# A decode attention kernel: P stored head by head, P V over tokens 64 apart, a row sum moved by one place, and a new order of the last projection

## Chip, cores and metric

The kernel runs on one core of a Trainium2 chip. The metric is the device time in microseconds (us) of one execution. A program on one core gives no second die to compare with, so the state of a run is judged against the fastest run of the same kernel.

## The reference, cut to what matters

Eight tokens (B = 8) each attend to 4096 cached positions in 32 heads of size 128; beside that runs a small MLP, and a gate mixes the two.

```python
q = (x @ wq).reshape(B, 1, 32, 128).transpose(0, 2, 1, 3)
scores = einsum("bhqd,bhkd->bhqk", q, k_cache) * 128 ** -0.5
p = softmax(scores); o = einsum("bhqk,bhkd->bhqd", p, v_cache)
a = o.transpose(0, 2, 1, 3).reshape(B, 1, 4096) @ wo
b = gelu(layernorm(x) @ w1 + b1) @ w2 + b2
out = g * a + (1 - g) * b          # g = sigmoid(sum(x * gate_w))
```

K and V are 268 MB each in bf16; with the weights the kernel reads 557 MB.

## The kernel before

The work is cut into 32 groups (8 heads of one batch entry). A group's K is 8.4 MB: 128 partitions (16 for each of 8 heads) with 256 tokens of 128 values, 64 KB a partition. V is the same. There are three slots of that size in the on-chip memory; the loads go round them in the order K0, K1, V0, K2, V1, K3, V2, ... A load is issued when the slot it needs has been given up.

In the profiles PE is TensorE (PEld its weight loads), DVE is VectorE, ACT is ScalarE, and SP is the engine that issues the loads. For each group DVE multiplies K by q in 8 chunks; TensorE sums each chunk over the head size (8 matmuls with the identity per chunk, into PSUM); DVE reduces the rest. Then a short chain of DVE operations finds the maxima, ScalarE does 8 exps (one per head, with a bias that leaves only that head's own partitions above zero), and 64 matmuls form P V with the weights P (4 tokens x 8 heads = 32 columns) and V (4 tokens x 128) as the moving operand. P V of group g - 1 stands in TensorE's order after the scores of group g. Then three short steps follow: gather (TensorE adds up the row sums and the parts of the four tokens), norm (DVE divides by the row sum) and, after every fourth group, turn (TensorE transposes O for the projection with wo).

```python
HB = 8; NTT = 256; TQ = 4; NTQ = NTT // TQ        # heads, tokens per partition, tokens per matmul
P = sb("P", [128, NTT, HB], BF16)

# softmax(g), its last part
for h in range(HB):
    a_exp[g] = op("scalar", lambda e, h=h: e.activation(
        out=P[:, :, h], in_=s_sb[:, s, :], func=ACT.Exp, bias=hb8[:, h:h + 1], scale=1.0),
        [v_nm[g], p_pv.get(g - 1), v_rs.get(g - 1)])

def rowsum(g):       # DVE: sum of P over 2048 elements a partition; waits for the exps
    v_rs[g] = op("vector", lambda e: e.tensor_reduce(out=rr[...], in_=P[:, :, :]..., ...), [a_exp[g], ...])

def pv(g):
    for tq in range(NTQ):
        w = [land["v", g], a_exp[g], ...] if tq == 0 else ()
        p_pv[g] = op("tensor", lambda e, o=o, tq=tq: e.matmul(
            o, lhsT=P[:, tq * TQ:(tq + 1) * TQ, :].rearrange("p t h -> p (t h)"),
            rhs=vb[:, tq * TQ:(tq + 1) * TQ, :].rearrange("p t d -> p (t d)"), ...), w)

for g in range(NG):
    def between(c, g=g):                  # called after the multiply of chunk c
        if g >= 1 and c == 1:
            rowsum(g - 1)
        if g >= 2:                        # gather, norm (and every fourth group turn) of g - 2
            ...
    scores(g, between)                    # mult 0, mult 1, then: reduce c, mult c + 2
    free[n_of["k", g]] = [p_sum[g, NCK - 1]]      # K's slot: free after its last sums
    next_load() if g < NG - 1 else load_wo(...)   # this is where V of group g is issued
    if g >= 1:
        pv(g - 1)
        free[n_of["v", g - 1]] = [p_pv[g - 1]]
        next_load()                               # K of group g + 2
    softmax(g)
    ...
# ... cut ...
rowsum(last); pv(last); evict(last)
for m in range(6):                        # 96 of the 128 matmuls of the projection
    ...quarters(OT[:, m, r, :], wo_sb[:, m, ...], ...)
gather(last); norm(last); turn(last // 4)
for m in range(6, WM):                    # the other 32
    ...
```

Of the kernel before, what the change touches and what calls it, by code (L numbers as in the profile page):

```python
# [5 lines left out]
ACT = mybir.ActivationFunctionType  # L6
ALU = mybir.AluOpType
AX = mybir.AxisListType
BF16 = mybir.dt.bfloat16
F32 = mybir.dt.float32  # L10

B = 8
D = 576
H = 32
DH = 128
# [6 lines left out]
HB = 8  # L22
# [3 lines left out]
NTT = SK // PH  # L26
# [4 lines left out]
TQ = 4  # L31
NTQ = NTT // TQ
# [5 lines left out]
WM = H // 4  # L38
WR = 4
# [51 lines left out]
def bass_gated_mix__mha_block_cached__mixer_channel_mlp__decode_kernel(  # L91
# [16 lines left out]
    sb = nc.alloc_sbuf_tensor  # L108
    S = Stream(nc)
    op = S.op  # L110
# [21 lines left out]
    wo_sb = view(SL, WO_SLOT * SLOT, [128, WM, WR * D])  # L132
# [43 lines left out]
    OT = sb("OT", [128, WM, WR, B], BF16)  # L176
# [3 lines left out]
    ident = sb("ident", [128, 128], BF16)  # L180
    hsel = sb("hsel", [128, HB], F32)
    hneg = sb("hneg", [128, HB], F32)
    sel32 = sb("sel32", [128, TQ, HB], F32)
    stat = sb("stat", [B, 16], F32)
    s_sb = sb("s_sb", [128, 2, NTT], F32)
    mA = sb("mA", [128, 32], F32)
# [2 lines left out]
    mD = sb("mD", [128, 32], F32)  # L189
    gm = sb("gm", [128, 2], F32)  # L190
    hb8 = sb("hb8", [128, HB], F32)
    P = sb("P", [128, NTT, HB], BF16)
    rr = sb("rr", [128, 2], F32)
    O_sb = sb("O_sb", [128, TQ, DH], F32)
    rz = sb("rz", [128, 1], F32)
# [6 lines left out]
    oz_ps = bank[5]  # L202
# [71 lines left out]
    def own_head(t, inside, outside):  # L274
# [9 lines left out]
    c_ps = [memset("vector", bank[i][:, :], 0.0) for i in (0, 1, 4, 5, 6)]  # L284
    c_yps = memset("vector", y_ps[:, :], 0.0)
    c_sel32 = op("vector", lambda e: e.tensor_reduce(
        out=sel32[:].rearrange("p t h -> p (t h)"),
        in_=bass.AP(tensor=ident, offset=0, ap=[[pstride(ident), 128], [1, TQ * HB], [32, 4]]),
        axis=AX.X, op=ALU.add), [c_id])
    c_Sel = op("vector", lambda e: e.tensor_copy(  # L290
        out=Sel[:].rearrange("p b (h r) -> p b h r", h=4),
        in_=bass.AP(tensor=ident, offset=0, ap=[[pstride(ident), 128], [1, B], [32, 4], [0, PH]])), [c_id])


    t = op("vector", lambda e: e.tensor_reduce(out=stat[:, 0:1], in_=x_sb, axis=AX.X, op=ALU.add), [ld_x])
    t1 = op("vector", lambda e: e.tensor_tensor_reduce(out=junk, in0=x_sb, in1=x_sb, scale=1.0, scalar=0.0,
                                                       op0=ALU.mult, op1=ALU.add, accum_out=stat[:, 1:2]))
    t = op("vector", lambda e: e.tensor_scalar(out=stat[:, 2:3], in0=stat[:, 0:1], scalar1=1.0 / D, scalar2=None,
                                               op0=ALU.mult), [t])
    t = op("vector", lambda e: e.tensor_tensor(out=stat[:, 3:4], in0=stat[:, 2:3], in1=stat[:, 2:3], op=ALU.mult), [t])  # L300
# [33 lines left out]
    t = op("vector", lambda e: e.reciprocal(out=stat[:, 7:8], in_=stat[:, 5:6]), [a_sqrt])  # L334
# [13 lines left out]
    for half in range(2):  # L348
        for h in range(4):
            for kt in range(NKT):  # L350
                o = tr_ps[half][32 * h:32 * h + B, :]
# [51 lines left out]
    def quarters(lhsT, w, first, stop, waits):  # L403

        for i in range(4):
            last = op("tensor", lambda e, i=i: e.matmul(  # L406
                y_ps[32 * i:32 * i + B, 0:QN], lhsT=lhsT, rhs=w[:, i * QN:(i + 1) * QN], start=first, stop=stop),
                waits if i == 0 else ())
        return last
# [53 lines left out]
    def softmax(g):  # L463
        s = g % 2
        t = op("vector", lambda e: e.tensor_reduce(out=mA[:, 0:1], in_=s_sb[:, s, :], axis=AX.X, op=ALU.max),  # L465
               [v_red[g, NCK - 1], c_mA])
        t = op("vector", lambda e: e.transpose(mB[:, :], mA[:, :]), [t])
        t = op("vector", lambda e: e.tensor_reduce(out=gm[:, :], in_=mB[:, :].rearrange("p (k r) -> p k r", k=2),
                                                   axis=AX.X, op=ALU.max), [t])
        gmb = bass.AP(tensor=gm, offset=0, ap=[[pstride(gm), 128], [1, 2], [0, PH]])  # L470
        t = op("vector", lambda e: e.tensor_scalar(out=mC[:, :].rearrange("p (k r) -> p k r", k=2), in0=gmb,
                                                   scalar1=-1.0, scalar2=None, op0=ALU.mult), [t])
        t = op("vector", lambda e: e.transpose(mD[:, :], mC[:, :]), [t])
        v_nm[g] = op("vector", lambda e: e.tensor_scalar(out=hb8[:, :], in0=hneg[:, :], scalar1=mD[:, 0:1], scalar2=None,  # L474
                                                         op0=ALU.add), [t, c_hneg, a_exp.get(g - 1)])
        for h in range(HB):
            a_exp[g] = op("scalar", lambda e, h=h: e.activation(  # L477
                out=P[:, :, h], in_=s_sb[:, s, :], func=ACT.Exp, bias=hb8[:, h:h + 1], scale=1.0),
                [v_nm[g], p_pv.get(g - 1), v_rs.get(g - 1)])

    def rowsum(g):
        v_rs[g] = op("vector", lambda e: e.tensor_reduce(  # L482
            out=rr[:, g % 2:g % 2 + 1], in_=P[:, :, :].rearrange("p t h -> p (t h)"), axis=AX.X, op=ALU.add),
            [a_exp[g], p_z.get(g - 2)])

    def pv(g):
        s = g % 2
        vb = slot[at_slot["v", g]]
        for tq in range(NTQ):
            o = o_ps[s][32 * (tq % 4):32 * (tq % 4) + TQ * HB, :]  # L490
            w = [land["v", g], a_exp[g], a_ev.get(g - 2), *v_hT] if tq == 0 else ()
            p_pv[g] = op("tensor", lambda e, o=o, tq=tq: e.matmul(  # L492
                o, lhsT=P[:, tq * TQ:(tq + 1) * TQ, :].rearrange("p t h -> p (t h)"),
                rhs=vb[:, tq * TQ:(tq + 1) * TQ, :].rearrange("p t d -> p (t d)"),
                start=(tq < 4), stop=(tq >= NTQ - 4)), w)

    def evict(g):
# [6 lines left out]
    def gather(g):  # L504
        q = quad(g)
        p_z[g] = op("tensor", lambda e: e.matmul(  # L506
            oz_ps[q, DH:DH + 1], lhsT=hsel[:, :], rhs=rr[:, g % 2:g % 2 + 1], start=True, stop=True),
            [v_rs[g], v_norm.get(g - 4), c_hsel, *v_hb])
        for tt in range(TQ):
            p_oz[g] = op("tensor", lambda e, tt=tt: e.matmul(  # L510
                oz_ps[q, 0:DH], lhsT=sel32[:, tt, :], rhs=O_sb[:, tt, :], start=(tt == 0), stop=(tt == TQ - 1)),
                [a_ev[g], c_sel32] if tt == 0 else ())

    def norm(g):
        q = quad(g)
        t = op("vector", lambda e: e.reciprocal(out=rz[q, :], in_=oz_ps[q, DH:DH + 1]), [p_oz[g]])  # L516
        v_norm[g] = op("vector", lambda e: e.tensor_scalar(  # L517
            out=Orow[q, (g // 4) % 2, :], in0=oz_ps[q, 0:DH], scalar1=rz[q, 0:1], scalar2=None, op0=ALU.mult),
            [t, c_Or, p_tp.get(g // 4 - 2)])

    def turn(k):

        hg, b0 = divmod(4 * k, B)
        for r in range(WR):
            i = Orow[:, k % 2, r::WR]
            for h4 in range(4):
                p_tp[k] = op("tensor", lambda e, r=r, h4=h4, i=i: e.matmul(  # L527
                    tp_ps[32 * h4:32 * h4 + 32, r * 8:(r + 1) * 8], lhsT=i,
                    rhs=bass.AP(tensor=ident, offset=h4, ap=[[pstride(ident), 128], [4, 2], [32, 4]]),
                    start=True, stop=True), [v_norm[4 * k + 3], v_ot.get(k - 1), *v_hb] if r == h4 == 0 else ())  # L530
        v_ot[k] = op("vector", lambda e: e.tensor_copy(  # L531
            out=OT[:, 2 * hg:2 * hg + 2, :, b0:b0 + 4],
            in_=bass.AP(tensor=tp_ps, offset=0, ap=[[pstride(tp_ps), 128], [4, 2], [8, WR], [1, 4]])), [p_tp[k]])
# [20 lines left out]
    ld_wo = {}  # L554
# [10 lines left out]
    for g in range(NG):  # L565

        def between(c, g=g):
            if g >= 1 and c == 1:
                rowsum(g - 1)
            if g >= 2:  # L570
                if c == 2:
                    gather(g - 2)
                if c == 3:
                    norm(g - 2)
                if c == 4 and (g - 2) % 4 == 3:
                    turn((g - 2) // 4)
            if c == 5 and g + 1 < NG:
                q_of(g + 1)

        scores(g, between)  # L580
        free[n_of["k", g]] = [p_sum[g, NCK - 1]]
        if g < NG - 1:
            next_load()
        else:
            load_wo(free[n_of["k", g]])
# [3 lines that stand above are left out]
            next_load()  # L589
        softmax(g)  # L590
        if g >= 1:
            evict(g - 1)
    last = NG - 1
# [2 lines left out]
    rowsum(last)  # L596
    pv(last)
    evict(last)
    for m in range(6):
        for r in range(WR):  # L600
            p_a = quarters(OT[:, m, r, :], wo_sb[:, m, r * D:(r + 1) * D], m == r == 0, False,
                           [ld_wo[m, r], v_bx, *v_ot.values()])
    gather(last)
    norm(last)
    turn(last // 4)
    for m in range(6, WM):
        for r in range(WR):
            p_a = quarters(OT[:, m, r, :], wo_sb[:, m, r * D:(r + 1) * D], False, m == WM - 1 and r == WR - 1,
                           [ld_wo[m, r], v_ot[last // 4]])
    t = op("vector", lambda e: e.scalar_tensor_tensor(  # L610
        out=out_sb[0:QP, :], in0=y_ps[0:QP, 0:QN], scalar=g4[0:QP, 0:1], in1=bmg_sb[0:QP, :],
        op0=ALU.mult, op1=ALU.add), [p_a, v_bmg])
# [37 lines left out]
```

## Time and profile before

| | before |
|---|---|
| time, median of the first 3 runs | 1307.37 us (1307.22 to 1307.7) |
| bytes read, mean rate | 557.03 MB, 427 GB/s |
| share of the span in which the load queue was busy | 98.9% |
| busy: TensorE, DVE, ScalarE | 57%, 67%, 25% |

The page of the kernel before, from its part on DMA queues (packets, MB, share of 16 engines' span):

```profile
q1 hardware_dynamic: 11200, 556.93, 98.9%
HBM read 557.03 MB, written 0.01 MB: 427 GB/s over the span
```

The table by stretches, kernel before: the stretch in us and its length, busy us (and instructions) of PE, PEld, DVE, ACT and POOL, then the granted clock, the DMA share and GB/s.

```profile
122.00:1278.00 1156.00, 664.76 (x4270) 261.01 (x4266) 805.62 (x751) 301.94 (x299) 0.00 (x0) 0.85 1.00 433
...
114.00:116.00 2.00, 1.66 (x8) 0.70 (x8) 2.00 (x3) 0.00 (x0) 0.00 (x0) 1.00 1.14 492
116.00:118.00 2.00, 1.10 (x6) 0.41 (x5) 1.69 (x2) 0.00 (x0) 0.00 (x0) 1.00 0.00 0
118.00:120.00 2.00, 2.00 (x25) 0.85 (x27) 0.89 (x2) 0.00 (x0) 0.00 (x0) 1.00 0.00 0
120.00:122.00 2.00, 2.00 (x44) 0.97 (x36) 1.83 (x7) 0.00 (x0) 0.00 (x0) 1.00 1.52 524
```

The kernel is bound by its transfers, at 433 GB/s for over 1100 us, but there is one hole of 4 us near 116 us. (A packet is counted in the stretch in which it starts, so short stretches scatter around 433; only the zeros mean something: no packet started there.)

The timeline of the kernel before shows why. The lines are start, length, engine, source line, what; in brackets the idle time before it and what ended it. First ScalarE's 8 exps and DVE's row sum of group 0, then the load queue (SP): V of group 1 and K of group 3.

```profile
87.58 9.42 ACT L477 ACTIVATE P<-s_sb,hb 128x256 bf16<-128x256 f32 x8 [6.21 <-DVE hb L474]
97.03 2.29 DVE L482 TENSOR_REDUCE rr<-P 128x1 f32<-128x2048 bf16 x1 [5.09 <-ACT P L477]
...
119.07 0.33 SPq L259 DMA_DIRECT2D SL<-in_A_v_cache_dram  x1
122.65 0.33 SPq L259 DMA_DIRECT2D SL<-in_A_k_cache_dram  x1
```

DVE stands idle for 5.09 us because the row sum of group 0, which comes early in group 1, waits for the exps. That delays group 1, whose end releases the slot for V of group 1.

Later in the run the queue is never empty. The same view of the kernel before, 1000 us later (V, K, then the first multiply on a K that has just landed):

```profile
1160.52 0.33 SPq L259 DMA_DIRECT2D SL<-in_A_v_cache_dram  x1
1164.10 0.33 SPq L259 DMA_DIRECT2D SL<-in_A_k_cache_dram  x1
...
1172.74 4.50 DVE L437 TENSOR_TENSOR SL<-SL,q_bc 128x4096 bf16<-128x4096 bf16 x2 [9.87 <-DMA SL<-in_A_k_cache_dram]
```

A K that was asked for long before lands at 1172.7, 12 us after this V was issued: the queue holds some 10 us of work, and DVE waits for data.

The groups of instructions of the kernel before (line, engine, operation, operands, count, then busy us and mean ns of one, then idle us before it and what ended that):

```profile
L477 ACT ACTIVATE P<-s_sb,hb 128x256 bf16<-128x256 f32 x256 | 299.9, 1602 | 296.1 <-PE psb L492 289.9 <-DVE hb L474 6.2
L447 DVE TENSOR_REDUCE s_sb<-psb 128x32 f32<-128x512 f32 x256 | 174.7, 683 | 51.0 <-PE psb L442 50.2
L482 DVE TENSOR_REDUCE rr<-P 128x1 f32<-128x2048 bf16 x32 | 73.0, 2280 | 16.0 <-ACT P L477 15.9
L492 PEld LDWEIGHTS psb<-SL,P 128*32 128x32 bf16 x2048 | 54.2, 97 | 60.9 <-issue 13.1
L498 ACT ACTIVATE O_sb<-psb 128x512 f32<-128x512 f32 x32 | 29.0, 907 | 6.4 <-PE psb L492 6.4
```

Exps overlap each other, so 256 of them at 1602 ns are 299.9 us busy: 1.17 us each.

And the end of the kernel before, from its timeline: the turned O of the last groups, the last 32 matmuls of the projection and the final operation.

```profile
1301.06 0.19 DVE L531 CAST OT<-psb 128x32 bf16<-128x32 f32 x1 [0.41 <-PE psb L527]
1301.40 0.67 PE L406 MATMUL psb<-SL,OT 128*8 128x144 bf16 x32 [0.39 <-DVE OT L531]
1302.12 0.37 DVE L610 SCALAR_TENSOR_TENSOR out_sb<-psb,g,bmg_sb 104x144 bf16<-104x144 f32 x1 [0.87 <-PE psb L406]
```

wo is loaded in five pieces. The landing records of the trace put them at 1295.6, 1298.4, 1299.8, 1300.5 and 1301.24 us.

### The profile page before, as it was taken

What the parts mean: (1) busy time and instruction counts of PE and PEld (TensorE: products, weight loads), DVE (VectorE), ACT (ScalarE), POOL (GpSimd) and SP (SyncE); (2) the same over time, 40 slices, a digit from 0 to 9 for tenths busy, and PEclk for the clock granted to TensorE, in tenths of its full rate; (3) what the DMA queues carried; (4) which work ended last, traced back from release to release, by engine and by line L of the source; (5) the groups of instructions that cost most, each with busy time, mean ns of one, the idle gap of its engine ahead of it and who ended that gap; (6) DMA issues with size and microseconds to landing.
All of it is one profiled execution on the core that took longest, in us unless ns stands there. A gap on an engine that the chain in (4) does not pass through costs nothing.

```text
span 1305.3 us, 11677 instructions
## 1 busy us (share of the span) xinstructions
PE 739.7 (57%) x5136; PEld 302.2 (23%) x5136; DVE 880.3 (67%) x860; ACT 329.6 (25%) x330; POOL 3.8 (0%) x19
## 2 busy tenths in 40 slices
PE   3466575565565555566555556556556555556645
PEld 1322222221222221222222222222222222222213
DVE  3377777676677766668766668757668776667862
ACT  1032113333311323312223321223330233330223
POOL 1000000000000000000000000000000000000000
PEclk8598888888898888898787899787799788799878
DMA  9998999999999999999999999999999999999997
GB/s 392 437 440 376 436 432 433 433 432 434 428 440 426 437 432 432 436 426 441 422 443 424 441 424 437 430 438 426 440 424 441 424 440 427 438 431 432 432 436 299
DMA packets 11442, 557.78 MB, mean 427 GB/s; under 512 B 1360, under 2 KB 1376, under 8 KB 2816
## 3 DMA queue, kind: packets, MB, share of 16 engines
q1 hardware_dynamic: 11200, 556.93, 98.9%
q8 instruction: 40, 0.66, 0.2%
q10 hardware_dynamic: 192, 0.11, 0.0%
q14 instruction: 10, 0.08, 0.0%
HBM read 557.03 MB, written 0.01 MB: 427 GB/s over the span
## 4 chain that ended last, share of the span: by engine, by line
DMA 53%; DVE 30%; PE 13%; ACT 4%; issue 0%; SPq 0%; ACTq 0%
DMA SL<-in_A_k_cache_dram 51%; DVE SL L437 21%; PE psb L442 6%; PE psb L492 5%; DVE s_sb L447 5%; ACT P L477 4%; DVE rr L482 3%; DMA SL<-in_A_wo_dram 2%; PE psb L510 1%; DMA SL<-in_A_wq_dram 1%; DVE Orow L517 0%; PE psb L355 0%; DVE rz L516 0%; PE psb L506 0%; PE psb L406 0%
## 5 line engine op out<-in xcount | busy, mean ns | idle before, releaser
L442 PE MATMUL psb<-SL,ident 128*128 128x512 bf16 x2048 | 559.8, 426 | 521.4 <-DVE SL L437 521.4
L437 DVE TENSOR_TENSOR SL<-SL,q_bc 128x4096 bf16<-128x4096 bf16 x256 | 581.5, 2282 | 267.1 <-DMA SL<-in_A_k_cache_dram 255.3
L442 PEld LDWEIGHTS psb<-SL,ident 128*128 128x128 bf16 x2048 | 200.9, 107 | 855.2 <-DVE SL L437 608.2
L477 ACT ACTIVATE P<-s_sb,hb 128x256 bf16<-128x256 f32 x256 | 299.9, 1602 | 296.1 <-PE psb L492 289.9
L447 DVE TENSOR_REDUCE s_sb<-psb 128x32 f32<-128x512 f32 x256 | 174.7, 683 | 51.0 <-PE psb L442 50.2
L429 ACT ACTIVATE q_bc<-psb 128x128 bf16<-128x128 f32 x32 | 8.9, 278 | 631.9 <-PE psb L426 631.9
L492 PE MATMUL psb<-SL,P 128*32 128x512 bf16 x2048 | 118.2, 383 | 0.0
L482 DVE TENSOR_REDUCE rr<-P 128x1 f32<-128x2048 bf16 x32 | 73.0, 2280 | 16.0 <-ACT P L477 15.9
L492 PEld LDWEIGHTS psb<-SL,P 128*32 128x32 bf16 x2048 | 54.2, 97 | 60.9 <-issue 13.1
L510 PE MATMUL psb<-O_sb,sel 128*8 128x128 f32 x256 | 34.4, 279 | 9.9 <-ACT O_sb L498 9.9
L498 ACT ACTIVATE O_sb<-psb 128x512 f32<-128x512 f32 x32 | 29.0, 907 | 6.4 <-PE psb L492 6.4
L510 PEld LDWEIGHTS psb<-O_sb,sel 128*8 128x8 f32 x256 | 21.2, 91 | 14.5 <-ACT O_sb L498 10.0
L516 DVE RECIPROCAL rz<-psb 8x1 f32<-8x1 f32 x32 | 5.2, 164 | 27.8 <-PE psb L510 27.8
L465 DVE TENSOR_REDUCE mA<-s_sb 128x1 f32<-128x256 f32 x32 | 13.4, 420 | 1.1
L377 DVE TENSOR_TENSOR SL<-psb,SL 104x384 f32<-104x384 f32 x3 | 1.7, 551 | 18.4 <-PE psb L373 18.4
L531 DVE CAST OT<-psb 128x32 bf16<-128x32 f32 x8 | 1.5, 191 | 16.2 <-PE psb L527 16.2
L396 PE MATMUL psb<-ident,SL 8*32 8x8 bf16 x144 | 8.0, 195 | 7.5 <-DVE SL L387 7.5
L517 DVE TENSOR_SCALAR Orow<-psb,rz 8x128 bf16<-8x128 f32 x32 | 11.1, 347 | 1.1
L396 PEld LDWEIGHTS psb<-ident,SL 8*32 8x32 bf16 x144 | 7.9, 148 | 7.9 <-DVE SL L387 7.9
L373 PE MATMUL psb<-SL 128*8 128x384 bf16 x60 | 4.9, 460 | 6.7 <-DMA SL<-in_B_w_dram 6.7
L474 DVE TENSOR_SCALAR hb<-hneg,mD 128x8 f32<-128x8 f32 x32 | 7.4, 232 | 1.1
L426 PE MATMUL psb<-Q,Sel 128*64 128x128 bf16 x64 | 8.0, 247 | 0.0
(70 smaller groups left out, 96.9 us busy)
## 6 DMA issues: line engine op xcount, KB each, us to landing
SL<-in_B_w_dram SPq DMA_DIRECT2D x1, 5184.0 KB, 38.1
SL<-in_B_w_dram SPq DMA_DIRECT2D x1, 4608.0 KB, 24.7
SL<-in_A_wq_dram SPq DMA_DIRECT2D x1, 4096.0 KB, 13.2
SL<-in_A_wo_dram SPq DMA_DIRECT2D x1, 2304.0 KB, 18.0
SL<-in_A_wo_dram SPq DMA_DIRECT2D x1, 1152.0 KB, 20.4
SL<-in_B_w_dram SPq DMA_DIRECT2D x1, 576.0 KB, 25.7
SL<-in_A_wo_dram SPq DMA_DIRECT2D x1, 576.0 KB, 21.3
SL<-in_A_wo_dram SPq DMA_DIRECT2D x2, 288.0 KB, 21.6
```

The costliest lines, as they stand in the source:

```text
L396: p_hT = op("tensor", lambda e, o=o, i=i, c=c: e.matmul(o, lhsT=i, rhs=ident[32 * c:32 * c + B, 32 * c:32 * c + B], start=True, stop=True) ...
L429: a_qb[g] = op("scalar", lambda e: e.activation(out=q_bc[:, g % 2, :], in_=qb_ps[:, 0:DH], func=ACT.Copy), [t, v_mult.get((g - 2, NCK - 1))])
L437: v_mult[g, c] = op("vector", lambda e: e.tensor_tensor(out=part, in0=part, in1=qb, op=ALU.mult), [land["k", g], a_qb[g]])
L442: p_sum[g, c] = op("tensor", lambda e, r=r, n=n: e.matmul(tr_ps[par][:, :], lhsT=ident[:, :], rhs=r, start=(n == 0), stop=(n == NCH - 1)), w)
L447: v_red[g, c] = op("vector", lambda e: e.tensor_reduce(out=s_sb[:, s, c * CT:(c + 1) * CT], in_=tr_ps[par][:, :].rearrange("p (t c) -> p t ...
L465: t = op("vector", lambda e: e.tensor_reduce(out=mA[:, 0:1], in_=s_sb[:, s, :], axis=AX.X, op=ALU.max), [v_red[g, NCK - 1], c_mA])
L477: a_exp[g] = op("scalar", lambda e, h=h: e.activation(out=P[:, :, h], in_=s_sb[:, s, :], func=ACT.Exp, bias=hb8[:, h:h + 1], scale=1.0), [ ...
L482: v_rs[g] = op("vector", lambda e: e.tensor_reduce(out=rr[:, g % 2:g % 2 + 1], in_=P[:, :, :].rearrange("p t h -> p (t h)"), axis=AX.X, op ...
L492: p_pv[g] = op("tensor", lambda e, o=o, tq=tq: e.matmul(o, lhsT=P[:, tq * TQ:(tq + 1) * TQ, :].rearrange("p t h -> p (t h)"), rhs=vb[:, tq ...
L498: a_ev[g] = op("scalar", lambda e: e.activation(out=O_sb[:].rearrange("p t d -> p (t d)"), in_=o_ps[g % 2][:, :], func=ACT.Copy), [p_pv[g] ...
L510: p_oz[g] = op("tensor", lambda e, tt=tt: e.matmul(oz_ps[q, 0:DH], lhsT=sel32[:, tt, :], rhs=O_sb[:, tt, :], start=(tt == 0), stop=(tt == ...
L517: v_norm[g] = op("vector", lambda e: e.tensor_scalar(out=Orow[q, (g // 4) % 2, :], in0=oz_ps[q, 0:DH], scalar1=rz[q, 0:1], scalar2=None, o ...
```

## The change

The intent has three parts. The exps write contiguous runs (they wrote 2 bytes in every 16). P V then takes tokens tq, tq + 64, tq + 128, tq + 192 in one matmul, so that its weights are a plain stride through P. In the tail, half of wo is projected ahead of the last turn, after gather and norm of the last group. Besides, the row sum moves one place later in DVE's order.

```diff
-    P = sb("P", [128, NTT, HB], BF16)
+    P = sb("P", [128, HB, NTT], BF16)
@@ softmax
-                out=P[:, :, h], in_=s_sb[:, s, :], func=ACT.Exp, ...
+                out=P[:, h, :], in_=s_sb[:, s, :], func=ACT.Exp, ...
@@ pv
-                o, lhsT=P[:, tq * TQ:(tq + 1) * TQ, :].rearrange("p t h -> p (t h)"),
-                rhs=vb[:, tq * TQ:(tq + 1) * TQ, :].rearrange("p t d -> p (t d)"),
+                o, lhsT=P[:, :, :].rearrange("p h t -> p (h t)")[:, tq::NTQ], rhs=vb[:, tq::NTQ, :],
@@ between
-            if g >= 1 and c == 1:
+            if g >= 1 and c == 2:
                 rowsum(g - 1)
@@ tail
-    for m in range(6): ... quarters(...)          # 96 matmuls
     gather(last)
     norm(last)
+    a_proj(range(4), list(v_ot.values()))          # 64 matmuls
     turn(last // 4)
-    for m in range(6, WM): ... quarters(...)      # 32 matmuls
+    p_a = a_proj(range(4, WM), list(v_ot.values()))  # 64 matmuls
```

(`sel32`, which sums the four tokens of a head, changes its order in the same way, and the row sum reads P in its new order.)

More of the change, by code (lines that the diff above doesn't have):

```diff
@@ L182, in bass_gated_mix__mha_block_cached__mixer_channel_mlp__decode_kernel @@
     hneg = sb("hneg", [128, HB], F32)
-    sel32 = sb("sel32", [128, TQ, HB], F32)
+    sel32 = sb("sel32", [128, HB, TQ], F32)
     stat = sb("stat", [B, 16], F32)
@@ L286, in bass_gated_mix__mha_block_cached__mixer_channel_mlp__decode_kernel @@
     c_sel32 = op("vector", lambda e: e.tensor_reduce(
-        out=sel32[:].rearrange("p t h -> p (t h)"),
+        out=sel32[:].rearrange("p h t -> p (h t)"),
         in_=bass.AP(tensor=ident, offset=0, ap=[[pstride(ident), 128], [1, TQ * HB], [32, 4]]),
@@ L477, in softmax @@
             a_exp[g] = op("scalar", lambda e, h=h: e.activation(
-                out=P[:, :, h], in_=s_sb[:, s, :], func=ACT.Exp, bias=hb8[:, h:h + 1], scale=1.0),
+                out=P[:, h, :], in_=s_sb[:, s, :], func=ACT.Exp, bias=hb8[:, h:h + 1], scale=1.0),
                 [v_nm[g], p_pv.get(g - 1), v_rs.get(g - 1)])
@@ L482, in rowsum @@
         v_rs[g] = op("vector", lambda e: e.tensor_reduce(
-            out=rr[:, g % 2:g % 2 + 1], in_=P[:, :, :].rearrange("p t h -> p (t h)"), axis=AX.X, op=ALU.add),
+            out=rr[:, g % 2:g % 2 + 1], in_=P[:, :, :].rearrange("p h t -> p (h t)"), axis=AX.X, op=ALU.add),
             [a_exp[g], p_z.get(g - 2)])
@@ L510, in gather @@
             p_oz[g] = op("tensor", lambda e, tt=tt: e.matmul(
-                oz_ps[q, 0:DH], lhsT=sel32[:, tt, :], rhs=O_sb[:, tt, :], start=(tt == 0), stop=(tt == TQ - 1)),
+                oz_ps[q, 0:DH], lhsT=sel32[:, :, tt], rhs=O_sb[:, tt, :], start=(tt == 0), stop=(tt == TQ - 1)),
                 [a_ev[g], c_sel32] if tt == 0 else ())
@@ L598, in bass_gated_mix__mha_block_cached__mixer_channel_mlp__decode_kernel, with a_proj @@
     evict(last)
-    for m in range(6):
-        for r in range(WR):
-            p_a = quarters(OT[:, m, r, :], wo_sb[:, m, r * D:(r + 1) * D], m == r == 0, False,
-                           [ld_wo[m, r], v_bx, *v_ot.values()])
     gather(last)
     norm(last)
+    def a_proj(ms, turned):
+        for m in ms:
+            for r in range(WR):
+                at = quarters(OT[:, m, r, :], wo_sb[:, m, r * D:(r + 1) * D], m == r == 0, m == WM - 1 and r == WR - 1,
+                              [ld_wo[m, r], v_bx, *turned])
+        return at
+    a_proj(range(4), list(v_ot.values()))
     turn(last // 4)
-    for m in range(6, WM):
-        for r in range(WR):
-            p_a = quarters(OT[:, m, r, :], wo_sb[:, m, r * D:(r + 1) * D], False, m == WM - 1 and r == WR - 1,
-                           [ld_wo[m, r], v_ot[last // 4]])
+    p_a = a_proj(range(4, WM), list(v_ot.values()))
     t = op("vector", lambda e: e.scalar_tensor_tensor(
```

## The prediction

> **What bounds the kernel.** The transfers. The page gives 557.03 MB read, the load queue busy 98.9% of the span. The table by stretches gives 433 GB/s from 122 to 1278 us. The Trainium skill ("DMA: Bandwidth & Descriptors", Specifications) puts the fabric ceiling at 435 GB/s; the trace agrees to 0.5%. In the SP timeline V is issued at 1160.5 and K at 1164.1, while the earlier K lands at 1172.7: some 10 us of transfers are still queued when V is issued. Compute that gets a few us faster or slower per group is hidden there; DVE already waits 255 us in total for K (list of waits).
>
> Only places where transfers are below full rate can give time:
> 1. The start; untouched.
> 2. One hole. In 2 us stretches the DMA share is 0.00 from 116 to 120; from 110 to 122 us the rate is 289 GB/s: 12 x (1 - 289/433) = 4.0 us lost. K of group 1 gives up its slot only at 119.07. Its chain runs through group 0's 8 exps (87.58, 9.42 us), on which the first row sum waits (DVE idle 5.09 us before 97.03).
> 3. The tail. wo is issued at 1277.55, a piece lands at 1298.40; after that run 32 matmuls, gather, norm, turn, 32 matmuls, and the final op at 1302.12.
>
> **What the change does.**
> - Exps: eight take 9.4 us, 1.17 us apart, each writing 2 bytes per 16. The Trainium skill ("SBUF — State Buffer", Door 1: The DMA port swizzle) says lines are 16 bytes and each crossing costs; the 1.17 us agree. "ScalarE: Activation LUTs" (What ACT_TABLE_LOAD costs) gives 280 + 0.833 N ns less 93 overlap: 400 ns for N = 256. My estimate: 3.3 us for eight, ACT busy 330 to about 135 us.
> - P V: weights are now 32 columns 128 bytes apart. Before, 64 matmuls take 3.60 us. I expect 3.6 to 4.5 us; if the weight load suffers as the exps did, 7 to 8 us. The moving operand keeps runs of 256 bytes and should cost nothing.
> - Row sum (2.28 us): same length, later in DVE's order, so it no longer waits.
> - Tail: gather and norm of the last group go ahead of all wo matmuls; 64 instead of 96 before the last turn, 64 instead of 32 after it.
>
> **On the critical path.** In the steady state nothing. In the hole: group 1 moves up by 3.5 to 5 us, its V is issued at 114 to 116 instead of 119.07: 3.2 to 4 us won, once. In the tail: the last P V waits for V instead of the exps; gather, norm and turn hide behind wo's landing, leaving 64 matmuls (1.4 us) after it instead of the 3.7 us chain: 1.5 to 2 us won. Sum: about 5.3 us of 1307.4, **1302.1 us**, range 1299 to 1305 (8 in 10). Faster by over 2%: 0.01; within 2%: 0.97; slower by over 2%: 0.02.
>
> **What would show it.** ACT busy near 135 us; steady load rate still 433 GB/s, K landings still about 39 us apart; ACT's saved time becomes idle time; no empty DMA stretch near 116 to 120; final op within 2 us of the last wo landing.
>
> **What would make it wrong.** A strided weight load that doubles P V: hidden in the steady state, but it would eat the tail's gain (about 1304). Exp writes that did slow the transfers: 5 us stretches show 410 to 419 GB/s just before the exps and 419 during them, so no. A P V over 10 us slower uses up the queue's slack, slows every group and exceeds the range.

## The result, and the profile after

| | before | changed |
|---|---|---|
| median | 1307.53 us (4 runs, 1307.22 to 1308.27) | 1304.53 us (4 runs: 1304.73, 1304.75, 1303.02, 1304.33) |
| ratio | | 0.9974, 95% interval 0.9956 to 0.9991 |

The ratio is the mean time of one kernel's fast runs over that of the other's of the same rounds, so not quite the ratio of the medians. It is clear of 1. The predicted range (1299 to 1305) holds the median; the predicted gain was 5.3 us, the measured one 3.0. Note that one run of the four lies apart from the others.

The groups of the changed kernel, in the order of those shown before:

```profile
L477 ACT ACTIVATE P<-s_sb,hb 128x256 bf16<-128x256 f32 x256 | 105.5, 494 | 302.8 <-PE psb L492 296.6 <-DVE hb L474 6.2
L447 DVE TENSOR_REDUCE s_sb<-psb 128x32 f32<-128x512 f32 x256 | 175.3, 685 | 94.6 <-PE psb L442 93.8
L482 DVE TENSOR_REDUCE rr<-P 128x1 f32<-128x2048 bf16 x32 | 72.9, 2279 | 0.0
L492 PEld LDWEIGHTS psb<-SL,P 128*32 128x32 bf16 x2048 | 89.9, 169 | 33.3 <-issue 15.7 <-DMA SL<-in_A_v_cache_dram 2.6
L497 ACT ACTIVATE O_sb<-psb 128x512 f32<-128x512 f32 x32 | 18.4, 575 | 9.4 <-PE psb L492 9.4
```

The exps fell from 299.9 to 105.5 us, the row sum waits for nothing, the weight loads of P V went from 97 to 169 ns each (up to four of them run at once, so they too are busy for less than count times mean). The second line is the one to remember: DVE's wait for the chunk sums rose from 50.2 to 93.8 us.

The same short stretches, the load queue, and the first multiply on K of group 3, all of the changed kernel (before, that multiply started at 161.31):

```profile
114.00:116.00 2.00, 2.00 (x19) 0.94 (x20) 0.61 (x2) 0.00 (x0) 0.00 (x0) 1.00 1.14 492
116.00:118.00 2.00, 2.00 (x44) 1.67 (x40) 1.73 (x7) 0.00 (x0) 0.00 (x0) 1.00 0.98 360
118.00:120.00 2.00, 1.19 (x24) 0.66 (x16) 1.38 (x1) 0.69 (x2) 0.00 (x0) 1.00 1.15 426
120.00:122.00 2.00, 1.03 (x5) 0.51 (x6) 2.00 (x2) 2.00 (x6) 0.00 (x0) 1.00 0.52 197
```

```profile
115.58 0.33 SPq L259 DMA_DIRECT2D SL<-in_A_v_cache_dram  x1
119.24 0.33 SPq L259 DMA_DIRECT2D SL<-in_A_k_cache_dram  x1
...
159.60 4.49 DVE L437 TENSOR_TENSOR SL<-SL,q_bc 128x4096 bf16<-128x4096 bf16 x2 [11.74 <-DMA SL<-in_A_k_cache_dram]
```

V of group 1 goes out 3.5 us earlier and there is no stretch any more in which no packet starts. Yet K of group 3, the load after it, lands only 1.7 us earlier (161.31 to 159.60), not 3.5 to 4. From there to K of group 31 the two kernels keep step: 161.31 to 1251.10 before, 159.60 to 1249.37 after, 1089.8 us for 28 groups in both. So the middle of the run gives nothing, as predicted, and the gain at the hole was 1.7 us.

The end of the changed kernel, from its timeline:

```profile
1298.71 0.30 PE L406 MATMUL psb<-SL,OT 128*8 128x144 bf16 x8 [0.29 <-DMA SL<-in_A_wo_dram]
1299.43 0.30 PE L406 MATMUL psb<-SL,OT 128*8 128x144 bf16 x8 [0.42 <-DMA SL<-in_A_wo_dram]
1299.78 0.37 DVE L611 SCALAR_TENSOR_TENSOR out_sb<-psb,g,bmg_sb 104x144 bf16<-104x144 f32 x1 [2.62 <-PE psb L406]
```

TensorE now waits for the last pieces of wo, whose last landing is at 1299.38. The final operation follows it by 0.40 us; before it was 1302.12 - 1301.24 = 0.88 us. So the tail's own gain is 0.5 us, not 1.5 to 2.

### The profile page after: what moved, and what is told of

Read it like the earlier page. It is cut to its first block, busy times and chain, and to the rows that moved or that the text cites. A ratio compares the mean times of both kernels' runs of the same rounds, so it can differ in the third digit from the quotient of the medians.

```text
span 1302.9 us, 11677 instructions
## 1 busy us (share of the span) xinstructions
PE 760.0 (58%) x5136; PEld 342.3 (26%) x5136; DVE 882.6 (68%) x860; ACT 136.9 (11%) x330; POOL 3.8 (0%) x19
## 4 chain that ended last, share of the span: by engine, by line
DMA 57%; DVE 28%; PE 15%; issue 0%; SPq 0%
DMA SL<-in_A_k_cache_dram 54%; DVE SL L437 19%; PE psb L442 10%; DVE s_sb L447 5%; PE psb L492 4%; DVE rr L482 3%; DMA SL<-in_A_wo_dram 2%; DMA SL<-in_A_wq_dram 1%; DVE Orow L516 0%; PE psb L355 0%; DVE rz L515 0%; SPq L214 0%; PE psb L526 0%; DVE OT L530 0%; DVE mA L465 0%
## 5 line engine op out<-in xcount | busy, mean ns | idle before, releaser
L442 PE MATMUL psb<-SL,ident 128*128 128x512 bf16 x2048 | 574.8, 435 | 501.6 <-DVE SL L437 495.1
L442 PEld LDWEIGHTS psb<-SL,ident 128*128 128x128 bf16 x2048 | 204.1, 109 | 847.1 <-DVE SL L437 592.9
L447 DVE TENSOR_REDUCE s_sb<-psb 128x32 f32<-128x512 f32 x256 | 175.3, 685 | 94.6 <-PE psb L442 93.8
L477 ACT ACTIVATE P<-s_sb,hb 128x256 bf16<-128x256 f32 x256 | 105.5, 494 | 302.8 <-PE psb L492 296.6
L492 PE MATMUL psb<-SL,P 128*32 128x512 bf16 x2048 | 121.0, 389 | 2.3 <-DMA SL<-in_A_v_cache_dram 2.3
L492 PEld LDWEIGHTS psb<-SL,P 128*32 128x32 bf16 x2048 | 89.9, 169 | 33.3 <-issue 15.7
L497 ACT ACTIVATE O_sb<-psb 128x512 f32<-128x512 f32 x32 | 18.4, 575 | 9.4 <-PE psb L492 9.4
L530 DVE CAST OT<-psb 128x32 bf16<-128x32 f32 x8 | 1.5, 192 | 19.8 <-PE psb L526 19.8
## 6 DMA issues: line engine op xcount, KB each, us to landing
SL<-in_A_wo_dram SPq DMA_DIRECT2D x1, 576.0 KB, 19.8
```

What stands on the lines that cost most here:

```text
L442: p_sum[g, c] = op("tensor", lambda e, r=r, n=n: e.matmul(tr_ps[par][:, :], lhsT=ident[:, :], rhs=r, start=(n == 0), stop=(n == NCH - 1)), w)
L447: v_red[g, c] = op("vector", lambda e: e.tensor_reduce(out=s_sb[:, s, c * CT:(c + 1) * CT], in_=tr_ps[par][:, :].rearrange("p (t c) -> p t ...
L477: a_exp[g] = op("scalar", lambda e, h=h: e.activation(out=P[:, h, :], in_=s_sb[:, s, :], func=ACT.Exp, bias=hb8[:, h:h + 1], scale=1.0), [ ...
L492: p_pv[g] = op("tensor", lambda e, o=o, tq=tq: e.matmul(o, lhsT=P[:, :, :].rearrange("p h t -> p (h t)")[:, tq::NTQ], rhs=vb[:, tq::NTQ, : ...
L497: a_ev[g] = op("scalar", lambda e: e.activation(out=O_sb[:].rearrange("p t d -> p (t d)"), in_=o_ps[g % 2][:, :], func=ACT.Copy), [p_pv[g] ...
```

## The experiments

### Which part of the change gives the gain

The first theory (A): the gain at the hole is what the slowest of the 16 DMA engines was idle, since a load lands when the last engine is done. In the packet records the first engine finishes K of group 2 near 116.2 us and the last near 118.2 in both kernels, and the next packets start at 120.0 before. That leaves 1.8 us of idle time for the last engine, close to the 1.7 us seen. Rivals: the tail's order gives the gain (B); the whole hole counts (C); the old exps' scattered writes slowed the transfers (D).

The changed kernel once more, as a yardstick, unedited.

> The changed kernel once more, as the yardstick for its parts. All theories: 2 to 4 us below before (ratio 0.997 to 0.9985).

Measured: 1303.18 us median (1302.83, 1304.49, 1304.36, 1303.18, 1302.86), before 1307.82 (9 runs), ratio 0.9969 (0.9955 to 0.9982). That is 4.6 us by the medians, a little over the 2 to 4 expected, because the single runs stand at two levels, near 1303.0 and near 1304.4, and here three of five took the lower.

The layout alone, with row sum and tail as before:

```diff
+    P head by head, exps, P V and sel32 as in the change
             if g >= 1 and c == 1:            # row sum as before
     ...                                      # tail as before
```

> Before, with P head by head and the P V token order alone; row sum and tail stay as before. Theory A (the gain is the closed hole near 116 us, sized by the slowest DMA engine, about 1.7 us; the exps free the first row sum): V of group 1 issued near 115.5 instead of 119.07, K of group 3 landing 1.7 us earlier, time 1.5 to 2.5 us below before. Rival B (the gain comes from the tail's order): within 0.5 us of before. Rival D (the old exps' scattered writes slow the transfers): gain grows through the steady state, K landings under 38.70 us apart.

Measured: 1303.29 us median, 1303.25 to 1303.37 in all five rounds, ratio 0.9965 (0.9953 to 0.9978). That is 4.5 us below before: more than theory A allowed, as much as the whole change at its faster level, and without a second level. Rivals B and D fall here: the tail is the old one, and K of group 3 to K of group 31 takes 157.75 to 1247.54, again 1089.8 us.

The row sum alone, then the tail alone:

```diff
-            if g >= 1 and c == 1:
+            if g >= 1 and c == 2:            # only_rowsum: before with this line alone
```

> Before, with the row sum one place later and nothing else; the exps stay slow (9.4 us for eight). Theory A: the row sum meets exps that are nearly done, DVE idles under 1.5 us instead of 5.1 in group 1, V of group 1 issued at 115 to 117, so most of the 1.7 us is won with no change of layout. Rivals B and D: no gain (within 0.5 us).

Measured: 1307.29 us median (1305.64 to 1307.44), ratio 0.9992 (0.9979 to 1.0004). V of group 1 was issued at 116.40 and K of group 3 came at 158.97, 2.3 us earlier than before, so the hole did shrink. But the slow exps now bound the tail: the last piece of wo landed at 1298.77 and the final operation came only at 1301.18. From K of group 3 to the end this run took 1306.05 - 158.97 = 1147.1 us, before 1306.98 - 161.31 = 1145.7: of the 2.3 us won at the hole, 1.4 were lost again, in the tail. So theory A's forecast was met at the hole but missed in the time, of which only 0.5 us is won by the medians.

> Before, with the new order of the tail alone. Theory A: the last piece of wo lands at 1301.2 as before, the final operation follows it by 0.4 us instead of 0.9, so 0.3 to 0.6 us won. Rival B: 2 us or more won, as my prediction had for the tail (1.5 to 2).

Measured (before with the tail of the change): 1308.01 us median (1307.93 to 1308.31), ratio 1.0002 (0.9989 to 1.0014). Neither the 0.3 to 0.6 us of theory A nor the 2 us of rival B. The end of this run's timeline:

```profile
1301.48 0.19 DVE L531 CAST OT<-psb 128x32 bf16<-128x32 f32 x1 [0.56 <-PE psb L527]
1301.82 1.17 PE L406 MATMUL psb<-SL,OT 128*8 128x144 bf16 x64 [0.41 <-DVE OT L531]
1303.05 0.37 DVE L612 SCALAR_TENSOR_TENSOR out_sb<-psb,g,bmg_sb 104x144 bf16<-104x144 f32 x1 [1.37 <-PE psb L406]
```

With slow exps the turn comes last: its result is ready at 1301.67, after wo's last landing at 1301.51, and the new order leaves 64 matmuls (1.17 us) after it instead of 32 (0.67). The new order pays only once the exps are fast.

The changed kernel with the old tail:

```diff
+    (96 wo matmuls, gather, norm, turn, 32 wo matmuls, as before)
```

> The changed kernel with the old order of the tail (96 wo matmuls, then gather, norm, turn, 32). Theory A: as fast as the changed kernel within 0.7 us, since the last P V starts 3.7 us earlier and the chain ends near the landing of the last wo piece either way. Rival B: 2 us slower than the changed kernel, as slow as before within 1 us.

Measured: 1305.01 us median (1305.01, 1305.53, 1303.85, 1303.38, 1305.39), ratio 0.9976 (0.9962 to 0.9989). It has two levels as well, near 1303.6 and near 1305.3. Its time from the start of K of group 3 to the end (1305.01 - 159.48 = 1145.5 us) equals that of the layout alone (1303.29 - 157.75 = 1145.5); the changed kernel has 1304.73 - 159.60 = 1145.1. So by these profiles the tail's order is worth 0.4 us with fast exps (by the two levels 0.6 to 0.9, on another chip; theory A allowed 0.7), and the rest is decided before K of group 3.

### How much a hole costs, and what the steady state hides

Both edits make one load wait for one thing more; the waits are on things that come anyway.

```diff
+                ld_v1[1].append(p_pv[0])     # hole_back: V of group 1 also waits for P V of group 0
+            ld_v1[1].append(a_exp[1])        # hole_wider: ... for the exps of group 1
```

> The changed kernel, but V of group 1 is issued only after P V of group 0, at about 119.2 instead of 115.6: the hole is put back, everything else keeps its gain. Theory A (slowest engine counts): 1.5 to 2.2 us slower than the changed kernel. Theory C (the whole hole counts, as my prediction had it): 3.5 us slower. Rival B: no change.

Measured: issued at 119.60, 1306.22 us median (1305.59 to 1307.54), ratio 0.9991 (0.9978 to 1.0004). This is 1.7 us above the changed kernel's upper level (near 1304.5) and 3.3 above its lower one (near 1302.9), so it supports A or C according to which level is taken. It shows, with everything else of the change in place, that the hole carries the gain.

> The changed kernel, but V of group 1 is issued only after the exps of group 1, which themselves follow P V of group 0: about 122.7, a delay of 7.1 us. Theory A: the first 1.7 us of the delay are hidden behind the slowest engine, the rest counts in full: 5 to 5.7 us slower than the changed kernel, and 3.4 us slower than with the delay of 3.6 us. Theory C: 7 us slower. Rival B: no change.

Measured: issued at 123.12, 1310.53 us median (1309.18 to 1310.74), ratio 1.0020 (1.0007 to 1.0032), slower than before. From 119.60 to 123.12 the load is 3.5 us later, K of group 3 is 3.5 us later (161.98 to 165.47), the time of the profiled run 3.3 us (1307.22 to 1310.53), the median 4.3 us. Once the queue has run dry, delay counts in full. Theory A's figure for the distance from the changed kernel (5 to 5.7 us) was missed: it is 6.0 from the upper level and 7.6 from the lower.

```diff
-        for h in range(HB):
+        for h in list(range(HB)) * (3 if 3 <= g < NG - 2 else 1):   # each exp waits for the one before
```

> The changed kernel with every exp of groups 3 to 29 done three times (each pass waits for the one before; about 12 us for a group instead of 3.3; the results are the same). Theory A: the steady state hides it, time as the changed kernel within 0.7 us, K landings still 38.70 us apart or a little over. A theory in which the shorter exps pay in every group: up to 27 x 9 = 240 us slower.

Measured: 1303.34 us median (1302.91 to 1304.26), ratio 0.9967 (0.9954 to 0.9979): no slower than the changed kernel. The group of exps in this run:

```profile
L478 ACT ACTIVATE P<-s_sb,hb 128x256 bf16<-128x256 f32 x688 | 349.6, 508 | 322.0 <-PE psb L493 294.3 <-DVE hb L474 6.2
```

ScalarE did 432 exps more and was busy 381.1 us, more than before the change (329.6), for nothing lost: K of group 3 to K of group 31 took 1089.6 us. The saving of some 190 us on ScalarE is worth nothing in the groups that this run covers.

### Two levels, and the row sum's part in them

Theory A has fallen: at the lower level the whole hole is won. The table orders the profiled runs by the time at which V of group 1 was issued. (The profiled run of the kernel before, 1306.98 us, lies a little under its other runs, 1307.22 to 1308.35.)

| run | V of group 1 issued | first multiply on K of group 3 | time of that run |
|---|---|---|---|
| layout alone | 113.48 | 157.75 | 1303.29 |
| changed, second time | 114.52 | 157.69 | 1302.83 |
| exps three times | 114.99 | 157.86 | 1303.44 |
| changed | 115.58 | 159.60 | 1304.73 |
| changed with old tail | 115.65 | 159.48 | 1305.01 |
| row sum alone | 116.40 | 158.97 | 1306.05 |
| before | 119.07 | 161.31 | 1306.98 |
| tail alone | 119.19 | 161.74 | 1308.22 |
| hole put back | 119.60 | 161.98 | 1307.22 |
| hole wider | 123.12 | 165.47 | 1310.53 |

There is a step between 115.0 and 115.6. Theory E: V must be issued early enough to be under way before the engines run out of K of group 2 (their last packets end between 116.2 and 118.2); then the loads follow each other without loss. The packet records of these runs give the place of the step: where the engines had run dry, the first packet of V starts 0.95 to 0.97 us after its issue (116.40 to 117.36, 119.07 to 120.04), and the first engine has no packet of K left at 116.0 to 116.4. So an estimate from these numbers says that V must be issued by 115.1 to 115.5. And it is the moved row sum that puts the changed kernel beside this step. The DVE timeline of the changed kernel, start of group 1:

```profile
93.61 0.69 DVE L447 TENSOR_REDUCE s_sb<-psb 128x32 f32<-128x512 f32 x1 [1.49 <-PE psb L442]
94.22 2.28 DVE L437 TENSOR_TENSOR SL<-SL,q_bc 128x4096 bf16<-128x4096 bf16 x1
96.42 2.28 DVE L482 TENSOR_REDUCE rr<-P 128x1 f32<-128x2048 bf16 x1
```

and of the layout alone, where the row sum is early:

```profile
92.42 2.28 DVE L482 TENSOR_REDUCE rr<-P 128x1 f32<-128x2048 bf16 x1
94.62 0.68 DVE L447 TENSOR_REDUCE s_sb<-psb 128x32 f32<-128x512 f32 x1
```

After the first two multiplies DVE must wait for TensorE's first sums in any case. With fast exps an early row sum fills that wait; moved, it leaves a hole of 1.49 us there and comes later in full. The groups of the layout alone show it for the whole run: DVE waits neither for the exps nor longer for the sums (49.3 us, against 50.2 before and 93.8 in the changed kernel).

```profile
L447 DVE TENSOR_REDUCE s_sb<-psb 128x32 f32<-128x512 f32 x256 | 174.7, 682 | 49.9 <-PE psb L442 49.3
L482 DVE TENSOR_REDUCE rr<-P 128x1 f32<-128x2048 bf16 x32 | 72.9, 2278 | 0.0
```

Four runs on one chip test this. The rivals: the levels come from the chip (F); the row sum's place acts in every group, not through this load (G).

```diff
-            if g >= 1 and c == 2:                       # rowsum_early: the changed kernel,
+            if g >= 1 and c == 1:                       #   row sum back at its old place
-            if g >= 1 and c == 2:                       # rowsum_first_only:
+            if g >= 1 and c == (1 if g == 1 else 2):    #   back in group 1 alone
+            ld_v1[1].append(v_nm[1])                    # v_late: rowsum_early, but V of group 1
                                                         #   also waits for the maxima of group 1
```

> The changed kernel with the row sum back at its old place (layout and tail kept). Theory E (V of group 1 must be issued before the queue runs dry near 116; the moved row sum costs 1 to 2 us of that margin because it no longer fills DVE's wait for the first sums): V issued near 113.5, landing 19.4 us after the K before it, 1302.5 to 1303.1 in all rounds, without the changed kernel's second level near 1304.5. Rival F (the two levels come from the chip, not from the issue): both levels again.

> The changed kernel with the row sum early in group 1 alone. Theory E: as the first run of this call, 1302.5 to 1303.1 in all rounds. Theory G: as the changed kernel.

> As the first run of this call, but V of group 1 also waits for the head maxima of group 1, so that it is issued near 115.8 instead of 113.5; the row sum stays early. Theory E: 1304.2 to 1305.2 in all or nearly all rounds, V landing 20.5 to 22 us after the K before it. Theory G (the row sum's place matters in every group, not through this one load): as the first run, under 1303.2.

> The changed kernel once more, on the same chip as the other three. Theory E: single runs at two levels, near 1303.0 and near 1304.5, according to whether V of group 1 is issued by 115.0 or at 115.6. Rival F: the same two levels in the three other kernels too.

| run | V of group 1 issued | K of group 3 | all five times, us |
|---|---|---|---|
| rowsum_early | 112.94 | 158.08 | 1303.23, 1302.92, 1302.73, 1302.55, 1302.86 |
| rowsum_first_only | 113.48 | 157.56 | 1302.61, 1302.84, 1302.9, 1302.77, 1302.83 |
| v_late | 116.22 | 159.48 | 1304.26, 1304.27, 1304.01, 1303.82, 1304.29 |
| after_third (changed) | 116.05 | 159.53 | 1304.58, 1304.61, 1304.68, 1302.69, 1304.38 |

The load queue of rowsum_early and then of v_late:

```profile
112.94 0.33 SPq L259 DMA_DIRECT2D SL<-in_A_v_cache_dram  x1
```

```profile
116.22 0.33 SPq L259 DMA_DIRECT2D SL<-in_A_v_cache_dram  x1
```

Theory E holds. The row sum early in group 1 alone is as good as early everywhere, so G falls. One load issued 3.3 us later brings the upper level back in all five rounds with the row sum early, and on the same chip the two kernels that issue it by 113.5 show one level, so F falls for them. (v_late was expected at 1304.2 at least; two rounds are a little under.) The ratios to before are 0.9963 for both kernels with the early row sum and 0.9974 for the other two. Those intervals overlap; the single runs do not, except for the changed kernel's one run at the lower level.

rowsum_early, with a median of 1302.86 us, beats before by 4.6 us and the changed kernel of the same call by 1.7. By the single runs it is the better version, and rowsum_first_only (1302.83) is as good.

What puts a run of the changed kernel on one side or the other seems to be how fast TensorE's sums come: in the profile with V issued at 115.58 DVE waits another 0.81 us for sums at 105.10 us; in the one with 114.52 it does not. The clock that TensorE was granted from 102 to 104 us goes with it: 0.50 in the profiles with V issued at 115.58, 115.65 and 116.05 (waits of 0.81 to 0.89 us) and in the one at 114.99 (0.62 us), 1.00 in the one at 114.52. In the four profiles with the row sum early in group 1 and fast exps it is 1.00 as well. This is read from profiles; no run tested it.

A load issued at 115.6 to 116.4 costs 1.3 to 2.3 us although its first packets start within about a microsecond of the first engine running out. (By the landing records V of group 1 lands 19.3 to 19.5 us after K of group 2 where V was issued by 113.5 or at 114.5, 19.8 us after it where at 115.0, and 20.6 to 21.6 us after it in these runs.) In the packet records of the changed kernel at the upper level the first packets of this V mostly take 2.5 to 3.3 us instead of 2.42; at the lower level nearly all take 2.42. From 114 to 135 us the idle time of the engines and what their packets took above 2.42 us add up, per engine, to 1.2 to 1.9 us in the late runs, to 0.1 to 0.5 us with V issued by 115.0, and to 3.9 us in the kernel before (3.2 of them idle). That is most of the cost; the rest would fit a load that lands only when its last engine is done. What stays open is why the packets after a pause take longer: no run took that apart. Nor was it settled why the kernel with the hole put back and the one with the row sum alone also scatter by about 2 us.

## Why the prediction was right or wrong, point by point

- "In the steady state nothing": right. 28 groups take 1089.8 us before and after, and three times the exps cost nothing measurable.
- Exps 3.3 us for eight, ACT busy about 135 us: 3.30 us and 136.9 us. The Trainium skill's formula ("ScalarE: Activation LUTs", What ACT_TABLE_LOAD costs) agrees: 400 ns estimated, 105.5 / 256 = 412 ns measured. The lines of 16 bytes ("SBUF — State Buffer", Door 1: The DMA port swizzle) fit the 1.17 us of the scattered writes in direction; the page gives no size.
- P V 3.6 to 4.5 us: 3.72 us in the steady state (3.64 before). The weight loads became 74% longer (97 to 169 ns) and stayed hidden.
- Row sum, "so it no longer waits": right, but the other half was missed. DVE's wait for the sums rose by 43.6 us, and at the start of group 1 this pushed the one load that matters later.
- "Its V is issued at 114 to 116 instead of 119.07: 3.2 to 4 us won": the term that was mis-sized. That interval contains a step. Measured at K of group 3: 161.31 - 157.69 = 3.6 us when V was issued at 114.52, and 1.7 us when it was issued at 115.58. The changed kernel gets the one or the other.
- "1.5 to 2 us won" in the tail: mis-sized. With fast exps the new order is worth 0.4 to 0.5 us. The prediction took the landing at 1298.40 as the end of wo's transfers; that is the second of five pieces, and the last lands at 1301.24. In the old tail the final operation already started 0.88 us after it.
- The sum: 5.3 us predicted. At the lower level the changed kernel gains about 4.7 us (near 1302.9 against 1307.6), at the upper one about 3.1. The terms as measured add up to the profiled runs: 3.6 + 0.5 us at the lower level (1306.98 - 1302.83 = 4.15) and 1.7 + 0.5 at the upper one (1306.98 - 1304.73 = 2.25). The median of 1304.53 lies in the range, but in part by luck: the range held every gain from 2.4 to 8.4 us, and the prediction did not foresee two levels.

## What to carry to other kernels

When transfers bound a kernel, look for the few places where the queue runs dry; compute matters there and nowhere else, and there the time that counts is when the next load is issued, with a margin, not how much idle time a stretch shows. Before moving an operation because it waits, check whether it was filling a wait that exists anyway: speeding up what it waits for may be enough, and here the layout alone gave 4.5 us, while the move took up to 1.7 back. When single runs stand at two levels, find the event that lies beside a threshold and push it off.

## What the Trainium skill lacked or had wrong

- "DMA: Bandwidth & Descriptors" gives a fixed cost per transfer and a first-byte latency, but not what a late issue costs between large loads that follow each other. Here: nothing with V issued by 114.5 us (the K before it landed at 118.5 to 119.0), 0.5 us when it was issued at 115.0, 1.3 to 2.3 us when it was issued at 115.6 to 116.4, and every further microsecond in full from 119.6 on (3.5 us later, 3.5 us lost).
- "TensorE: Matmul & The Clock Gate" (LDWEIGHTS) makes the time of a weight load depend on the number of columns alone. With 32 columns in both kernels a load took 97 ns with the columns adjacent and 169 ns with them 128 bytes apart. (The lines of 16 bytes cited above point that way.)
- "SBUF — State Buffer" (Summary: rules for kernel authors) tells to use about 358 GB/s for loads from HBM. This core, running alone, read 433 GB/s for over 1100 us. "HBM Reference" does say that a core alone reads faster, about 425 GB/s.
- No page that I found says that scattered writes on ScalarE lengthen the operation after them: the eviction of O right after the exps took 907 ns before and 575 ns after, with the same operands. The one eviction of the kernel before that followed no exp at once, the last, took 597 ns.
